# Block-causal attention in front of an MoE and an MLP: from one head in 128-query tiles to two heads in 64-query tiles

## The chip, the cores and the metric

The kernel runs on one core of a Trainium2 chip. The metric is the device time of one launch in microseconds (us). Seven queues of work matter here: PE (TensorE matmuls and transposes) with PEld (its weight loads), DVE (VectorE), ACT (ScalarE), POOL (GpSimd), SP (which only issues DMAs here) and the DMA engines. Each engine executes its own instructions in the order in which the program gives them to it.

## The reference

Attention over 4 batches, 8 heads, 576 positions and 64 columns a head, masked by blocks of 64 positions, then a top-2 MoE over 8 experts, then a gated MLP:

```
B, H, S, D = q.shape                      # 4, 8, 576, 64
scores = 1/sqrt(D) * q @ k^T
mask = (pos[:, None] // 64) >= (pos[None, :] // 64)
scores = where(mask, scores, -1e9);  scores -= max(scores)
attn = exp(scores);  attn /= sum(attn) + 1e-9
x = (attn @ v) -> [B*S, H*D] = [2304, 512]
logits = x @ w_gate + log1p(exp(x @ w_noise)) * noise;  top 2 experts, softmax
out[t] += w * relu(x[t] @ w1[e]) @ w2[e]  # E=8, 512 -> 1024 -> 512
h = x @ w_in;  y = (h * clip(h + 3, 0, 6) / 6) @ w_out    # 512 -> 2048 -> 512
```

## The kernel before

Only the attention stage is changed; it takes about the first 266 us. The MoE and the MLP that follow it are the same text in both kernels.

Values that must be kept close to full fp32 are split in two parts of reduced fp32 (type fp32r), hi = rounded value and lo = value - hi, so that one product is the sum of several fp32r matmuls.

**Unit of work.** Heads come in 16 pairs (two heads of a batch, 128 columns side by side in DRAM), but nearly everything runs head by head. A head's 576 queries are cut in five tiles, `QC`: one of 64 queries and four of 128. A tile sees keys up to its own end: 64, 192, 320, 448, 576.

**q and k.** `hi` and `lo` (L593, L653) split the raw tile of both heads into [hi 64 | lo 64] columns of each head. `prep` (L664 to L671) transposes them on PE, so that hi lies on partitions 0 to 63 and lo on 64 to 127: 20 transposes a pair. `prep_out` (L593, L597) copies PSUM to SBUF (`qk`), on ACT. A swapped copy of q, [lo | hi], called `qw`, is made by two DMAs from POOL's queue (`swap`, L710 and L711); for the first pair PE makes it (`swap_nat`, `swap_prep`).

**Scores** (`scores`, L728). With 128 partitions holding hi and lo, two matmuls (`qk` and `qw` against the same k) give all four products hi*hi, lo*lo, lo*hi, hi*lo. Per head there are 12 matmuls, one or two tiles at a time into the PSUM buffers sb0 and sb1 (units `UN`).

**Mask.** Of a tile of 128 queries, the first 64 must not see the last 64 keys: a DVE memset of -1e30 (L928, four a head) overwrites this corner in PSUM.

**Softmax and P.** `rowmax` (L742, DVE) reduces each tile's scores, `expo` (L749, ACT) writes exp to `P` with the row sums in `rs`. `ptrans` (L767, PE) transposes `P` in 128 x 128 pieces, 15 a head; `pt_hi` (L593, mostly ACT) and `pt_lo` (L786, DVE) split the result into `pth` and `ptl`.

**Output.** `av` (L801, PE) multiplies by v (split by L593 and L653), `av_out` (L593, ACT) copies to `oT`, `fin` (L823, PE) transposes back by a matmul with the identity beside w_gate and w_noise, so that 80 columns come out: 64 of x and 16 of router logits. `x_out` (L831, DVE) divides by the row sum, `lsum` (L842, POOL) adds up the logits over the heads, `store_x` (SP) writes x to DRAM. After the last head of a batch `route` runs some 40 small steps, mostly on DVE.

**The order.** A list scheduler (`Plan`) sets the order in which instructions stand on each engine. `add(engines, fn, deps, prio)` gives a step its possible engines with an assumed cost each, its dependences and a due time; the dictionary `PR` holds the offsets of the due times. Buffers of PSUM (five banks `tb`, sb0, sb1) are handed out by the scheduler. A second plan (`plan2`) follows with the first expert on the first 256 tokens (`s1`, `s2`, L381 to L383), whose x rows were gathered early; it overlaps with the routing of the last batch.

Of the kernel before, what the change touches and what calls it, by code (L numbers as in the profile page):

```python
# [7 lines left out]
F32 = mybir.dt.float32  # L8
# [26 lines left out]
PR = {'split': -19.53, 'prep': -8.13, 'step': 1.69, 'keep': 1, 'S': -0.89, 'max': -12.96, 'exp': 0.81, 'pt': 3.19, 'hi': -5.56, 'lo': -5.14, 'hid': True, 'av': -6.36, 'o': 6.06, 'inv': 0.97, 'fin': 8.98, 'x': -8.39, 'route': 17.77, 'rp': 1, 'route2': 3.35, 'xt': 12, 'eg': 523.9, 'ex': 470.0, 'ew': 2084, 'es': 2041, 'first': 0, 'vpt': (0, 0, 0, 0, 0), 'vhi': (0.8, -0.59, 0.53, -1.31, 2.34), 'vlo': (0.76, -0.19, -0.9, -0.32, -0.13), 'vmax': (0, -1.99, 0, -3.15, 0), 'vexp': (-0.19, 0.18, -0.24, -0.26, -0.46), 'vav': (0.39, 0.71), 'vo': (0.12, -0.03), 'dav': (0.67, 1.02), 'df': 0.98, 'dpt': (0.27, 0.33, 0.44, 0.44, 0.11), 'ds': (0.34, 0.29, 0.4, 0.49), 'sel': 2, 'vh': 0, 'wl': 2, 'wa': 8.24, 'wb': 12.71, 'h': -29.8, 's2': 0.04, 'mask': (1, 2, 3, 4), 'u': (1.2, -1.27, 1.89, -1.62), 'od': True, 'qd': False, 'qa': False}  # L35
# [96 lines left out]
def kernel(  # L132
# [51 lines left out]
    def load(p, nm):  # L184
        src, big, sm, o = {"q": (q, slice(1, NC), 0, BLK), "k": (k_in, slice(0, NC - 1), NC - 1, 0),
                           "v": (v, slice(0, NC - 1), NC - 1, 0)}[nm]
        b, j = pairs[p]
        t = raw[nm, p % 2]
        hs = src[b, 2 * j:2 * j + 2]
        for i in range(2):  # L190
            nc.sync.dma_start(t[:, big, i], hs[i, o:o + S - BLK, :].rearrange("(c p) d -> p c d", p=128))
        r = 0 if o else S - BLK
        nc.sync.dma_start(t[:BLK, sm], hs[:, r:r + BLK, :].rearrange("h p d -> p h d"))

    for nm, pad in (("q", 0), ("k", NC - 1)):
        nc.vector.memset(raw[nm, 0][64:, pad], 0.0)
        load(0, nm)
# [214 lines left out]
    sqk_p = gctx.enter_context(tc.tile_pool(name="sqk", bufs=2, side="right", reuse_waits="tile"))  # L412
# [160 lines left out]
    with actx:  # L573
# [851 lines left out]
```

## Time and profile before

| | us |
|---|---|
| median of 3 runs (1142.65 to 1144.06) | 1144.01 |
| profiled execution | 1144.68 |
| its span, first to last instruction | 1142.9 |
| attention: last `fin` ends | about 266 |

The engines were busy for these shares of the span: PE 98%, DVE 70%, ACT 50%, POOL 25%. Busy time of PE holds the modelled drain of each matmul, so a PE that is 98% busy has hardly a gap, but the duration of one matmul is not what it costs: matmuls overlap. What one costs in a row of matmuls is the distance from its start to the start of the next.

### The profile page before, as it was taken

The numbers are of one execution on the slowest core, as the hardware profiler recorded it, in microseconds if no ns is written. First come the engines' busy times: TensorE is split into PE (matmuls) and PEld (weight loads), VectorE is DVE, ScalarE is ACT, GpSimd is POOL, SyncE is SP. The second block draws the span as 40 slices with busy tenths as digits, with TensorE's granted clock in tenths as the row PEclk, the third lists the DMA queues.
The fourth block names the chain that finished last, engine by engine and source line by source line (L and its number), as shares of the span: only waits on it lengthen the run. The fifth ranks groups of instructions, "written<-read, shape, count | busy, mean of one in ns | idle before, by whom it ended". The sixth has DMA issues, their size and how long they took to land. (4 is left out here: it accounts for less than half of the span.)

```text
span 1142.9 us, 18252 instructions
## 1 busy us (share of the span) xinstructions
PE 1122.8 (98%) x6652; PEld 988.6 (87%) x6652; DVE 803.7 (70%) x1659; ACT 565.9 (50%) x1179; POOL 282.7 (25%) x301
## 2 busy tenths in 40 slices
PE   8999999998999999999999999899999999999998
PEld 6899999997889999999999989788888888888887
DVE  7988999998468788787788775577645554554542
ACT  5888888885442323232323234555444444443442
POOL 5545555435611010101010000275320320200000
PEclk8999999999999999999999999999999999999999
DMA  6865564220697666766655422422101110100000
GB/s 132 199 152 128 130 157 111 64 61 22 223 335 260 246 238 224 250 229 193 205 172 187 172 100 77 155 74 75 46 28 37 29 46 19 38 1 1 38 1 37
DMA packets 134340, 139.71 MB, mean 122 GB/s; under 512 B 67816, under 2 KB 97512, under 8 KB 134248
## 3 DMA queue, kind: packets, MB, share of 16 engines
q1 hardware_dynamic: 118568, 100.30, 28.0%
q0 software_dynamic: 8480, 28.78, 9.2%
q10 hardware_dynamic: 7200, 9.44, 2.3%
q8 instruction: 53, 0.87, 0.3%
q14 instruction: 39, 0.32, 0.1%
HBM read 92.94 MB, written 36.70 MB: 113 GB/s over the span
## 5 line engine op out<-in xcount | busy, mean ns | idle before, releaser
L381 PE MATMUL h<-xh,wah 128*128 128x312 f32 (+5 forms) x832 | 279.9, 336 | 2.9 <-DVE hl L407 2.8
L383 PE MATMUL h<-xh,wal 128*128 128x312 f32 (+5 forms) x832 | 275.1, 331 | 0.0
L382 PE MATMUL h<-xl,wah 128*128 128x312 f32 (+5 forms) x832 | 275.1, 331 | 0.0
L1061 PE MATMUL y<-wbh,hh 128*128 128x512 f32 (+1 forms) x608 | 237.6, 391 | 2.6 <-issue 2.1
L1062 PE MATMUL y<-wbl,hh 128*128 128x512 f32 (+1 forms) x608 | 238.1, 392 | 0.2
L1063 PE MATMUL y<-wbh,hl 128*128 128x512 f32 (+1 forms) x608 | 237.3, 390 | 0.0
L381 PEld LDWEIGHTS h<-xh,wah 128*128 128x128 f32 x832 | 157.5, 189 | 15.2 <-DVE hl L407 3.2
L382 PEld LDWEIGHTS h<-xl,wah 128*128 128x128 f32 x832 | 157.6, 189 | 11.4
L383 PEld LDWEIGHTS h<-xh,wal 128*128 128x128 f32 x832 | 157.5, 189 | 10.3
L1063 PEld LDWEIGHTS y<-wbh,hl 128*128 128x128 f32 (+1 forms) x608 | 113.3, 186 | 25.6 <-DVE hl L1357 0.3
L1061 PEld LDWEIGHTS y<-wbh,hh 128*128 128x128 f32 (+1 forms) x608 | 113.4, 187 | 24.4 <-issue 2.6
L1062 PEld LDWEIGHTS y<-wbl,hh 128*128 128x128 f32 (+1 forms) x608 | 113.3, 186 | 22.3 <-POOL wbl L331 0.8
L404 ACT ACTIVATE hh<-h 128x312 fp32r<-128x312 f32 (+4 forms) x128 | 55.2, 431 | 146.5 <-PE h L383 145.9
L1354 DVE SCALAR_TENSOR_TENSOR r<-r,h 128x512 f32<-128x512 f32 (+1 forms) x80 | 50.5, 632 | 108.6 <-ACT r L1353 108.3
L1353 ACT ACTIVATE r<-h,three 128x512 f32<-128x512 f32 (+1 forms) x80 | 51.6, 644 | 125.8 <-PE h L383 125.8
L1225 POOL DMA_INDIRECT ga<-y_tab,slot x32 | 38.4, 1200 | 294.4 <-PE y L1063 113.7
L1039 POOL DMA_INDIRECT xn<-x_tok,ids x38 | 40.2, 1059 | 268.4 <-PE xps L344 263.9
L331 DVE TENSOR_TENSOR wal<-wa,wah 128x1024 fp32r<-128x1024 f32 x75 | 93.2, 1242 | 16.6 <-ACT wah L327 14.5
L749 ACT ACTIVATE P<-sb,nm 128x320 f32<-128x320 f32 (+4 forms) x160 | 84.8, 531 | 24.4 <-DVE nm L742 20.1
L347 ACT CAST xh<-xps 128x512 fp32r<-128x512 f32 x56 | 32.6, 587 | 127.3 <-PE xps L344 124.7
L331 DVE TENSOR_TENSOR wbl<-wb,wbh 128x1024 fp32r<-128x1024 f32 x71 | 86.5, 1219 | 12.9 <-ACT wbh L327 11.3
L1357 DVE TENSOR_TENSOR hl<-r,hh 128x512 fp32r<-128x512 f32 (+1 forms) x80 | 56.3, 703 | 51.5 <-ACT hh L1356 51.0
(238 smaller groups left out, 1983.1 us busy)
## 6 DMA issues: line engine op xcount, KB each, us to landing
wa<-in_moe_w_dram SPq DMA_DIRECT2D x23, 512.0 KB, 5.4
wb<-in_moe_w_dram SPq DMA_DIRECT2D x23, 512.0 KB, 8.2
qw<-qk POOLq DMA_DIRECT2D x30, 288.0 KB, 4.2
y_tab<-yo SPq DMA_DIRECT2D x32, 256.0 KB, 4.1
w<-in_moe_w_in_dram SPq DMA_DIRECT2D x16, 512.0 KB, 6.7
y_tab<-zero SPq DMA_DIRECT2D x8, 1024.0 KB, 10.9
w<-in_moe_w_out_dram SPq DMA_DIRECT2D x16, 512.0 KB, 5.5
wa<-in_moe_w_dram ACTq DMA_DIRECT2D x9, 512.0 KB, 9.4
```

The lines of the kernel that those rows point to most:

```text
L331: (nc.gpsimd if e == "POOL" else nc.vector).tensor_tensor(lo, raws[PS[u]][which], hi.bitcast(F32), op=OP.subtract)
L381: nc.tensor.matmul(ps, lhsT=wh, rhs=xh, start=first, stop=False)
L382: nc.tensor.matmul(ps, lhsT=wh, rhs=xl, start=False, stop=False)
L383: nc.tensor.matmul(ps, lhsT=wl, rhs=xh, start=False, stop=last)
L404: nc.scalar.activation(h[0][:, c0:c1], ps[:, :c1 - c0], AF.Relu)
L749: nc.scalar.activation(o, views.pop((hd, c)), AF.Exp, bias=nms.pop((hd, c))[:n], scale=1.0, accum_out=rs[hd % 3][:n, c:c + 1])
L1061: nc.tensor.matmul(yps[t][:n], lhsT=hh[:, sl], rhs=wh[:, f % 2], start=first, stop=False)
L1062: nc.tensor.matmul(yps[t][:n], lhsT=hh[:, sl], rhs=wl[:, f % 2], start=False, stop=False)
L1063: nc.tensor.matmul(yps[t][:n], lhsT=hl[:, sl], rhs=wh[:, f % 2], start=False, stop=last)
L1353: nc.scalar.activation(r[:, :n], ps[:, :n], AF.Relu, bias=three, scale=1.0)
L1354: nc.vector.scalar_tensor_tensor(r[:, :n], r[:, :n], 6.0, ps[:, :n], op0=OP.min, op1=OP.mult)
L1357: nc.vector.tensor_tensor(hl[:, :n], r[:, :n], hh[:, :n].bitcast(F32), op=OP.subtract)
```

## The change

The unit becomes a block of 64 queries of both heads of a pair: 128 rows, head 0 in the first 64, head 1 in the last. There are nine blocks a pair, and block i sees 64 (i + 1) keys, so no mask is left.

- q and k: the raw tile of two heads is transposed as it is, unsplit: 10 transposes a pair (4 of q, 4 of k, 2 for the last 64 positions). `prep_out` writes fp32 `qs` and `ks`, on ACT or DVE. Then `q_hi`, `q_lo` split q onto a block diagonal `qd` (head h's 64 partitions, the other head's half of the columns zero; two instructions of 64 partitions each), and `k_hi`, `k_lo` split k. From the second pair on, all four are on POOL alone. The casts of raw q and k on DVE, POOL's subtractions of them and the DMA swap are gone.
- Scores: three matmuls (hi*hi, hi*lo, lo*hi) a block, both heads at once; block 8 in two halves. 30 matmuls a pair.
- P: 25 transposes a pair, nine tiles; `pth` and `ptl` become the tiles `pt`.
- `fin`: 9 matmuls of 96 columns a pair (64 of x, 16 of logits for either head). `lsum` keeps sums of either head's rows in `lgp`, two instructions of 64 partitions a pair; a new `lgm` adds the two halves by three matmuls with a half identity a batch, and `lg_out` copies the result for `route`.
- `store_x` writes 64 partitions by 9 blocks of 64 columns, twice a pair.
- New tiles: `qd`, zeroed by eight memsets on POOL at the start, and `half`. The first expert's weights are split into a pool of their own (`e_p`).
- All due times in `PR` are new.

Its core, with `PR` and the unchanged parts left out:

```diff
+        NB = S // BLK
+        UN = ((0, 1, 3), (2, 4), (5,), (6,), (7,), (8,))
+        PART = ((0, 4), (4, NB))
...
+        qd = [[one.tile([128, NB, 2, BLK], F32R, name=f"qd{i}{w}") for w in "hl"] for i in range(2)]
+        for i in range(2):
+            for t in qd[i]:
+                for h in range(2):
+                    nc.gpsimd.memset(t[64 * h:64 * h + 64, :, 1 - h].bitcast(F32), 0.0)
...
+            if part < 2:
+                for c in range(NC - 1):
+                    nc.tensor.transpose(ps[:, c * 128:(c + 1) * 128], flat("qk"[part], p, c), ident)
+            else:
+                for i, nm in enumerate("qk"):
+                    nc.tensor.transpose(ps[:, i * 128:(i + 1) * 128], flat(nm, p, NC - 1), ident)
...
+        def q_lo(e, p):
+            for h in range(2):
+                r = slice(64 * h, 64 * h + 64)
+                engine(e).tensor_tensor(qd[p % 2][1][r, :, h], qs[p][0][r].rearrange("p (i s) -> p i s", s=BLK),
+                                        qd[p % 2][0][r, :, h].bitcast(F32), op=OP.subtract)
...
-                    for a, kk in enumerate((t, w)):
-                        nc.tensor.matmul(ps[:n, half, o:o + hl], lhsT=kk[:, j, s0:s0 + n],
-                                         rhs=t[:, 2 + j, half * hl:(half + 1) * hl], start=(a == 0), stop=(a == 1))
+                    for a, (w, x) in enumerate(((qh, kh), (qh, kl), (ql, kh))):
+                        nc.tensor.matmul(ps[:, half_, o:o + hl], lhsT=w[:, i], rhs=x[:, ks_], start=(a == 0), stop=(a == 2))
...
+            last = (i1 - 1) // 2
+            for c in range(last + 1):
+                a = max(i0, 2 * c)
+                for w in ((0, 1) if c < last else (1, 0)):
+                    n = 2 * D if w == 0 or (i1 - a) * BLK >= 256 else D
+                    nc.tensor.matmul(o[:n, a - i0:], lhsT=vs[:, c, h, :n], rhs=pt[w][part][:, a - i0:, c, h * BLK:(h + 1) * BLK],
+                                     start=(c == 0 and w == 0), stop=(c == last and w == 0))
...
+            for i in range(i1 - i0):
+                nc.tensor.matmul(f[:, i], lhsT=oT[p, part][:, i].rearrange("p h s -> p (h s)"), rhs=iw[:, p % NP2],
...
+            e1 = {"DVE": 0.7, "ACT": 1.1} if p == 0 else {"POOL": 1.35}
+            e2 = {"DVE": 1.4} if p == 0 else {"POOL": 2.9}
+            f1 = {"ACT": 0.55, "DVE": 0.38} if p == 0 else {"POOL": 0.68}
+            f2 = {"POOL": 1.45, "DVE": 0.68} if p == 0 else {"POOL": 1.45}
...
+            k["qh", p] = add(e1, lambda e, p=p: q_hi(e, p), [outs[0], outs[2]] + sold, tp)
+            k["ql", p] = add(e2, lambda e, p=p: q_lo(e, p), [k["qh", p]], tp)
+            k["kh", p] = add(f1, lambda e, p=p: k_hi(e, p), [outs[1], outs[3]] + sold, tp)
+            k["kl", p] = add(f2, lambda e, p=p: k_lo(e, p), [k["kh", p]], tp)
```

`sold` holds the six score units of the pair two before, since `qd` has two buffers.

What stands on POOL for one pair in the middle of the stage, before (`sp_q`, `sp_k`, `sp_v` are the split tiles, L710 and L711 the swap's DMAs, L842 the logit sum):

```order
L593 CAST sp_v<-raw_v_76 128x10x64
L653 TENSOR_TENSOR sp_v<-raw_v_76,sp_v 128x10x64
L653 TENSOR_TENSOR sp_q<-raw_q_73,sp_q 128x10x64
L653 TENSOR_TENSOR sp_k<-raw_k_75,sp_k 128x10x64
L842 TENSOR_TENSOR lg_158<-lg_158,x 128x80
L710 DMA qw<-qk 64x1152
L711 DMA qw<-qk 64x1152
L842 TENSOR_TENSOR lg_158<-lg_158,x 128x80
```

And after the change, again on POOL for one pair (`qd0h`, `qd0l`, `kh`, `kl` are the split q and k after the transposes):

```order
L580 CAST sp_v<-raw_v_76 128x10x64
L580 CAST qd0h<-qs 64x9x64 x2
L808 TENSOR_TENSOR lgp_219<-lgp_219,x 64x144 x2
L684 TENSOR_TENSOR qd0l<-qs,qd0h 64x9x64 x2
L580 CAST kh<-ks 128x576
L648 TENSOR_TENSOR sp_v<-raw_v_76,sp_v 128x10x64
L692 TENSOR_TENSOR kl<-ks,kh 128x576
```

The split of q and k has moved behind the transposes, and its casts have moved from DVE to POOL.

At the start of the program POOL has this before (`pth`, `ptl` take memsets; `sp_v` of the first pair is the first subtraction):

```order
L621 MEMSET P_195 128x64
L625 MEMSET rs_197 64x1
L625 MEMSET rs_199 64x1
L625 MEMSET rs_201 64x1
L629 MEMSET pth 64x128
L629 MEMSET ptl 64x128
L653 TENSOR_TENSOR sp_v<-raw_v_76,sp_v 128x10x64
L653 TENSOR_TENSOR sp_q<-raw_q_73,sp_q 128x10x64
```

and after, in the same place on POOL (`kl` in the third row from the end belongs to the first pair):

```order
L612 MEMSET qd1l 64x9x64 x2
L617 MEMSET P_194 128x64
L617 MEMSET P_197 128x64
L617 MEMSET P_200 128x64
L617 MEMSET P_203 128x64
L617 MEMSET P_206 128x64
L622 MEMSET half 128x192
L624 COPY half<-ident 64x64 x2
L648 TENSOR_TENSOR sp_v<-raw_v_76,sp_v 128x10x64
L692 TENSOR_TENSOR kl<-ks,kh 128x576
L580 CAST qd1h<-qs 64x9x64 x2
L580 CAST kh<-ks 128x576
```

The first pair's `kl`, which all its scores need, now stands on POOL behind the memsets and behind `sp_v`; before, nothing that the first scores need was on POOL.

At the end of the stage PE has this before (`raw_k_74` holds early gathered token rows, `h` is the first expert's product):

```order
L344 MATMUL tb_178<-ident,raw_k_74 128x128 x4
L801 MATMUL tb_179<-pth,sp_v 128x256
L801 MATMUL tb_179<-ptl,sp_v 128x256
...
L823 MATMUL tb_180<-iw,oT_4128 64x80
L823 MATMUL tb_180<-iw,oT_4128 128x80 x2
L823 MATMUL tb_180<-iw,oT_4157 128x80 x2
L381 MATMUL h<-xh,wah 128x256
```

and this after:

```order
L790 MATMUL tb_174<-iw,oT_3572 128x96 x4
L790 MATMUL tb_172<-iw,oT_3566 128x96 x5
L337 MATMUL tb_175<-ident,raw_q_72 128x128 x4
L337 MATMUL tb_171<-ident,raw_k_74 128x128 x4
L813 MATMUL tb_173<-lgp_220,half 128x16
L814 MATMUL tb_173<-lgp_220,half 128x64
L815 MATMUL tb_173<-lgp_220,half 128x64
L366 MATMUL h<-xh,wah 128x256
```

The transposes of the early token rows have moved behind the last `fin`, directly ahead of the expert that needs them, and the three matmuls of `lgm` stand between.

## Rows read from the trace of the kernel before

**Rows 1.** Windows: us, busy us (instructions) of each engine, clock, DMA share, GB/s.
```profile
10.00:20.00 10.00, 8.17 (x50) 7.01 (x50) 9.64 (x25) 6.50 (x20) 7.46 (x6) 0.83 0.62 137
20.00:30.00 10.00, 8.34 (x58) 7.68 (x56) 7.51 (x19) 6.53 (x20) 4.38 (x5) 0.83 0.66 133
40.00:256.00 216.00, 214.01 (x1797) 200.79 (x1795) 196.20 (x642) 182.41 (x561) 109.25 (x148) 1.00 0.52 124
```
**Rows 2.** Groups by form, DVE in 40 to 256 us: count | busy, mean ns | idle.
```profile
L742 DVE TENSOR_REDUCE nm<-sb 128x1 f32<-128x576 f32 x28 | 21.0, 748 | 0.3
L928 DVE MEMSET sb<- 64x64 f32 x113 | 12.7, 112 | 11.7 <-PE sb L728 9.5 <-ACT oT L593 1.0
```
**Rows 3.** Timeline of PE, two heads: start us, us to the end, what.
```profile
152.69 0.28 PE L801 MATMUL tb<-pth,sp_v 128*128 128x256 f32 x1
152.81 0.28 PE L801 MATMUL tb<-ptl,sp_v 128*128 128x256 f32 x1
...
153.29 0.34 PE L801 MATMUL tb<-ptl,sp_v 128*128 128x256 f32 x2
153.47 0.27 PE L801 MATMUL tb<-pth,sp_v 128*128 128x128 f32 x1
153.57 0.20 PE L728 MATMUL sb<-qk 128*64 128x64 f32 x1
...
153.95 0.33 PE L801 MATMUL tb<-pth,sp_v 128*128 128x320 f32 x1
154.12 0.31 PE L801 MATMUL tb<-ptl,sp_v 128*128 128x320 f32 x1
154.27 0.27 PE L801 MATMUL tb<-pth,sp_v 128*128 128x256 f32 x1
...
154.98 0.29 PE L728 MATMUL sb<-qk 128*128 128x288 f32 x1
155.11 0.29 PE L728 MATMUL sb<-qk,qw 128*128 128x288 f32 x1
...
155.35 0.60 PE L664 MATMUL tb<-ident,sp_q 128*128 128x128 f32 x4
155.79 0.49 PE L767 MATMUL tb<-ident,P 128*128 128x128 f32 x3
...
156.32 0.36 PE L728 MATMUL sb<-qk,qw 128*128 128x448 f32 x1
156.52 0.60 PE L767 MATMUL tb<-ident,P 128*128 128x128 f32 x4
...
157.44 1.40 PE L823 MATMUL tb<-iw,oT 128*64 128x80 f32 x10
158.63 0.39 PE L728 MATMUL sb<-qk 128*128 128x320 f32 x1
```
**Rows 4.** Groups by form, POOL in 40 to 256 us.
```profile
L653 POOL TENSOR_TENSOR sp_v<-raw_v,sp_v 128x640 fp32r<-128x640 f32 x13 | 20.5, 1578 | 0.6
L842 POOL TENSOR_TENSOR lg<-lg,x 128x80 f32<-128x80 f32 x25 | 9.0, 359 | 13.8 <-DVE x L831 9.8 <-DVE sb L928 2.2 <-DMA raw_v<-in_v_dram 0.9
L593 POOL CAST sp_v<-raw_v 128x640 fp32r<-128x640 f32 x12 | 8.7, 722 | 11.9 <-PE tb L801 11.8
L520 POOL TENSOR_TENSOR rid<-ohs,bw 128x400 bf16<-128x400 f32 x6 | 5.1, 861 | 0.0
```
**Rows 5.** Timeline of the start, POOL and PE.
```profile
4.08 0.20 POOL L629 MEMSET pth<- 64x128 f32 x1
...
9.10 1.55 POOL L653 TENSOR_TENSOR sp_v<-raw_v,sp_v 128x640 fp32r<-128x640 f32 x1 [4.68 <-ACT sp_v L593]
9.75 0.42 PE L728 MATMUL sb<-qk 128*128 128x320 f32 x1
```
**Rows 6.** Timeline of the end of the attention stage: POOL, DVE, PE.
```profile
264.24 0.69 DVE L352 TENSOR_TENSOR xl<-tb,xh 128x512 fp32r<-128x512 f32 x1 [0.48 <-ACT xh L347]
...
266.14 2.42 POOL L331 TENSOR_TENSOR wal<-wa,wah 128x1024 fp32r<-128x1024 f32 x1 [1.88 <-ACT wah L327]
266.63 2.03 DVE L842 TENSOR_TENSOR lg<-lg,x 128x80 f32<-128x80 f32 x1
271.75 0.39 PE L381 MATMUL h<-xh,wah 128*128 128x256 f32 x1 [2.81 <-DVE hl L407]
```

More of the change, by code (lines that the diff above doesn't have):

```diff
@@ L724, in scores @@
                 nh = 1 if L <= 512 else 2
                 hl = L // nh
-                for half in range(nh):
-                    for a, kk in enumerate((t, w)):
-                        nc.tensor.matmul(ps[:n, half, o:o + hl], lhsT=kk[:, j, s0:s0 + n],
-                                         rhs=t[:, 2 + j, half * hl:(half + 1) * hl], start=(a == 0), stop=(a == 1))
-                        if a == 0 and c and c not in PR["mask"] and half == nh - 1:
-                            nc.tensor.matmul(ps[:n, half, o + hl - BLK:o + hl], lhsT=mneg, rhs=ones[0:1, 0:BLK],
-                                             start=False, stop=False)
@@ new lines, in x_out, with lsum @@
+        def x_out(g, p, part, cols=slice(0, FW)):
+            if p not in xt:
+                xt[p] = sm_p.tile([128, NB, FW], F32, tag="x", name="x", bufs=3)
+            i0, i1 = PART[part]
+            nc.vector.tensor_tensor(xt[p][:, i0:i1, cols], fview(g, part)[:, :, cols],
+                                    ri[p][:, i0:i1, None].to_broadcast([128, i1 - i0, cols.stop - cols.start]), op=OP.mult)
+        def lsum(e, p):
+            b, j = pairs[p]
+            for h in range(2):
+                r = slice(64 * h, 64 * h + 64)
+                t = xt[p][r, :, D + h * 2 * E:D + (h + 1) * 2 * E]
+                if j == 0:
+                    engine(e).tensor_copy(lgp[b % 2][r], t)
+                else:
+                    engine(e).tensor_tensor(lgp[b % 2][r], lgp[b % 2][r], t, op=OP.add)
@@ L850, in load_noise, with store_x @@
+        def store_x(p):
+            b, j = pairs[p]
+            for h in range(2):
+                d = (2 * j + h) * D
+                nc.sync.dma_start(x_tok[b * S:(b + 1) * S, d:d + D].rearrange("(i r) d -> r i d", r=BLK),
+                                  xt[p][64 * h:64 * h + 64, :, 0:D])
         def load_noise(b):
@@ L871 @@
                 add({"SP": 1.1}, lambda e, p=p: load_raw(RAWP.index(p) + 1), [k["L", "v", p]], u0 + 4)
[L872 to L883 removed]
+            vu = u0 + PR["v"]
@@ L957 @@
                 g = Bank("t", 1)
-                k["F", hd] = add({"PE": PR["df"]}, lambda e, g=g, hd=hd: fin(g, hd), [k["O", hd, 0], k["O", hd, 1]],
-                                 U + PR["fin"], take=g)
-                old = [k.get(("X", b - 2, r)) for r in range(NP2)] + [k.get(("ls", 8 * (b - 1) - 1))] if h == 0 else []
-                cut = D if last else 0
+                k["F", p, part] = add({"PE": 0.222 * n}, lambda e, g=g, p=p, part=part: fin(g, p, part),
+                                      [k["O", p, h, part] for h in range(2)], U + PR["fin"] + PR["vf"][part], take=g)
```

517 lines of the change are left out of this document (206 added, 311 removed).

## The prediction

> **What bounds the kernel now.** First the busy time of each engine by stretches [rows 1]. From 40 to 256 us, where the pairs follow one another without start or tail, PE is busy for 214 of 216 us at full clock, DVE for 196, ACT for 182, POOL for 109. Next, groups by form: a group that runs once a head has a count of 28 there (`rowmax` of the full 576 keys [rows 2]). So a head takes 216 / 28 = 7.71 us and a pair 15.43. Last, the timeline of PE [rows 3]: its rows overlap (a matmul that starts at 152.69 and lasts 0.28 is followed by one at 152.81), so what a matmul costs is the distance to the next start. The stage is bound by the number and width of PE's matmuls. DVE at 91% is the second, and POOL has 49% to spare. The stages behind the attention run the same text and are taken as unchanged.
>
> **The change part by part: PE in a pair.** Costs by distance of starts, from [rows 3]:
>
> - A transpose of 128 columns: 155.35 to 155.79 for four, 0.11 each. Of 64 columns: 0.06, the value that the low half of 128 leaves in 153.29 to 153.47 (0.18, less 0.12 for the 256 columns before it).
> - AV: 256 columns 0.12, 320 columns 0.17 and 0.15, 128 columns 0.10 and 0.06.
> - Scores: the tiles of 64 and 192 keys take 153.57 to 153.95 for four matmuls, 0.38; 288 keys 0.13; 448 keys 0.20; 320 keys 0.15.
> - `fin` is full fp32, and each of its five matmuls a head stands twice in the trace: ten take 157.44 to 158.63, 1.19.
>
> Before, per pair: preparation 16 x 0.11 + 4 x 0.06 = 2.0. Scores of a head 0.38 + 0.30 + 4 x 0.13 + 2 x 0.20 = 1.60, so 3.2. P 30 x 0.11 = 3.3. AV of a head 10 x 0.12 + 0.32 (two of 320) + 4 x 0.08 = 1.84, so 3.7. `fin` 2.4. Together 14.6; the 0.8 that is left of 15.43 is route, switches and small gaps, and I keep it.
>
> After: preparation 10 x 0.11 = 1.1. P 25 x 0.11 = 2.75. `fin` 9 matmuls, 18 rows of 0.119 = 2.14. Scores, three matmuls a block: 0.11 for 64, 128 and 192 keys, 0.12 for 256, 0.15 for 320, 0.175 for 384 (between its neighbours), 0.20 for 448, 0.23 for 512 (carried on), 0.26 for 576; sum 1.465, times three 4.40. AV of a head by the order: two of 256 columns, six of 320, two each of 192, 128 and 64, so 0.24 + 0.90 + 0.20 + 0.16 + 0.16 = 1.66, a pair 3.3. Together 13.7. The scores grow by 1.2; preparation, P, AV and `fin` shrink by 0.9, 0.55, 0.35 and 0.25. Net -0.85 a pair.
>
> Unknown is the 64-key score matmul with 128-wide weights and a start of its own: at 0.06 (the narrow one above) it saves 3 x 2 x 0.05 = 0.3 a pair more, at 0.13 it costs 0.2 more. I take 0.11, the transposes' value, since these too have 128-wide weights. `lgm` is three full fp32 matmuls a batch, so six rows, at 0.11 to 0.119 (the widths lie beside `fin`'s): 4 x 6 x 0.11 = 2.6 us. Sixteen pairs: -13.6 + 2.6 = -11, with -5 to -16 from the 64-key bounds and a tenth of the 0.8 a pair either way. I take -12.5, since fewer and larger steps (nine score blocks for ten tiles, no mask between scores and `rowmax`) leave fewer switches.
>
> The Trainium skill, "TensorE: Matmul & The Clock Gate", section "Back-to-back issue gap", gives 81 ns a matmul for 128 columns and 131 for 512 in a sustained stream. By it (linear between, an estimate) a pair would go from 11.1 to 10.0 and the stage would gain 15 us in place of 11. The rows show 110 ns for 128 columns and 200 for 448, and 15.4 a pair; the measurement decides, and the sum above uses it.
>
> **The other engines in a pair.** DVE loses eight masks a pair (four a head, 113 in 28 heads [rows 2]) of 0.112 = 0.9 us, two casts, one `rowmax`; its 14.0 a pair (196.2 / 14) falls to about 12.5, and ACT loses copies. That takes nothing off the end: it loosens the cover. POOL gains [rows 4]: v cast 0.72 and subtraction 1.58 stay; new are q's casts 2 x 0.65 and k's 0.65 (0.72 x 576 / 640), q's subtractions 2 x 1.42 and k's 1.42 (1.578 x 576 / 640), logit sums about 1.0 for two of 144 columns (0.359 for 80), and route's steps such as 0.861. Sum 9.5 + 1.2 = 10.7 a pair, against PE's 14.6. No trace shows an operation on 64 partitions of POOL with a block stride. Bounds: half of the full-width row, when partitions count (half of the 4.1 of q goes: 8.6 a pair), and 1.5 times it, for the stride (the blocks written are not contiguous), which gives 10.7 + 0.5 x 6.2 = 13.8 or, if all of POOL stretches likewise, 16.05. I take the row itself, since a cost per column is what the 640 and 80 columns on 128 partitions show. Then a pair's split takes 6.2 us in a row, of two pairs' 14.6 that it may be early (two buffers of `qd`): hidden. If that cover is gone, each pair costs what POOL exceeds PE by.
>
> **The start.** Before, the first score matmul comes at 9.75, beside POOL's first subtraction (9.10, 1.55 [rows 5]). After, all first-pair scores need `kl`, which stands on POOL behind that subtraction: 9.10 + 1.55 + 1.42 + 0.15 = 12.2, +2.5. Ahead of it stand the eight `qd` memsets of 64 x 576 (four rows of x2); a 64 x 128 one took 0.20 [rows 5], so they cost between 8 x 0.2 = 1.6 and, by columns, 8 x 0.9 = 7.2. POOL idled for 4.68 ahead of 9.10; I take 8 x 0.55 = 4.4, hidden; by columns first scores come at 13.6, +3.8. Against that: between 10 and 30 us PE started 50 + 58 = 108 matmuls at clock 0.83 [rows 1], where 10 us of the steady stretch hold 1797 / 21.6 = 83, so 58 fewer; at 0.12 each that is 7 us of fill. The change brings a longer run of scores a pair and no split ahead of the transposes; I give back 3 of these 7 (0 to 7). Start: +2.5 - 3 = -0.5, from +3.8 to -4.5.
>
> **The tail.** Eight token transposes (0.88), their copies on ACT and the 0.69 of `xl` on DVE [rows 6] move behind the last `fin`, with `lgm` and its copy ahead of route. Before, the expert's matmul at 271.75 followed 2.81 of idle time [rows 6], so part is hidden. Between -1 (all in that gap, the last pair shorter) and +5 (0.88 + 0.69 + copies + 0.66 of `lgm` + a wait for POOL of 2.42); I take +2. What waits there is DVE, in order: its logit sum took 2.03 us from 266.63 and ended at 268.66, with POOL's `wal` (266.14 + 2.42 = 268.56 [rows 6]), while the same operation took 0.359 on POOL [rows 4]. The Trainium skill, "SBUF — State Buffer", section "Who interferes with whom", calls the port pair that DVE and GpSimd share "an exclusive lock". The trace agrees with it there, and it speaks against more work on POOL: the waits that it would bring are part of the third case below.
>
> Sum: -12.5 - 0.5 + 2 = -11, so the profiled 1144.68 would become 1133.7; the profiled run lies 0.67 above the median, and against the median's 1144.01 it is 1133. I forecast **1133 us**.
>
> **The rivals.** *The bound stays on PE and shrinks* (the forecast): 1124 to 1139, from the bounds above without the far ends of POOL. For it speaks a PE that is 99% busy; against it, that DVE is at 91%, so more than 1.4 us a pair could not be taken off by PE alone.
>
> *POOL becomes the bound.* The q and k split of the next pair gates its scores, and PE waits at the first block of each pair. It reaches PE's 14.6 at 14.6 / 10.7 = 1.36 times my rows, and the old 15.43 at 1.44 times. At 1.5 times it is 16.05 a pair, (16.05 - 15.43) x 16 = +10, and the start's `kl` comes later too (nothing gained there): about 1154. For it: strided writes on half the partitions, and the six operations in a row. Against: the rows are for the same types, and POOL is idle for half the time now.
>
> *PE's gain turns into waits of its own.* Fewer score buffers' worth of steps in flight, and DVE in order: a `rowmax` behind an operation that is held by POOL keeps a score buffer 1.4 us (one subtraction) longer. Half of that once a pair, 0.7 x 16 = 11, eats the gain on PE: 1143, between 1138 and 1148. For it: POOL's share of time rises from 51% to 10.7 / 14.6 = 73%. Against: PE has other work (P, AV) to put there.
>
> *More is gained.* The 64-key matmuls go at 0.06 (-5), the fill is recovered whole (-4), and the tail costs nothing (-2), with half of the switches gone (-4): 1118, from 1110 to 1124. For it: 58 matmuls short in the fill. Against: each of these is the favourable end.
>
> **How the numbers follow.** Chances: forecast 0.54, POOL 0.18, waits 0.15, more 0.13. Within 0.2% (2.3 us, what a measurement of this kernel can tell from no change) lie 1141.7 to 1146.3. The forecast and the last case lie wholly on the faster side (0.67), the POOL case on the slower side (0.18); the waits split in 0.06 faster, 0.06 same and 0.03 slower. So faster 0.73, same 0.06, slower 0.21. The range 1117 to 1151 leaves out about a third of the last case and the larger half of POOL's; the likeliest case's own is 1124 to 1139.
>
> **What would show it.** Right: a pair in 14.3 to 14.9 us between 40 and 250 us, PE still over 97% busy there, POOL near 10.7 a pair with subtractions of 64 x 9 x 64 near 1.42, `kl` of the first pair ending near 12, first scores behind it, and the first expert matmul at 259 to 263. Wrong: those subtractions above 2.0 with PE idle ahead of the first score of a pair, released by POOL (the second case); PE idle in pieces under 1 us, released by DVE or by score buffers (the third); 64-key score matmuls at 0.06 (the fourth). A first score later than 14 us, or an expert matmul that comes over 9 us after the last `fin`, would put the error in the start or the tail.

## The result and the profile after

| | before | after |
|---|---|---|
| median of 4 runs, same chip | 1143.33 us (1141.16 to 1144.06) | 1131.46 us (1129.82 to 1132.65) |
| ratio | | 0.9898 (0.9877 to 0.9920) |
| profiled execution | 1144.68 us | 1132.54 us |
| last `fin` ends | 266.04 us | 251.06 us |
| first product of the expert's second weight, `y` | 276.21 us | 265.22 us |

The change takes 1.0% off: 11.9 us by the medians and 12.1 by the profiled executions, where 11 was forecast. The attention ends 15.0 us earlier, the stretch from there to the first `y` product is 4.0 us longer (14.2 for 10.2), and what follows is 1.1 shorter. The profiled execution is one of the slower two of the four runs (1132.5 and 1132.7 us at a mean granted clock of 0.987; the other two took 1129.8 and 1130.4 at 0.993).

The first `y` is not the same point in both orders: after the change the route's matmuls `rps` stand ahead of it, before they stood behind six `y` products. At the next point that both kernels reach with the same work done, the matmul `cps` of the MoE (336.03 us before, 325.55 after), PE is 10.5 us ahead, so that 4.5 of the 15.0 are lost by then. From `cps` to the end the same text took 803.0 to 806.9 us in the fourteen profiled executions of this document, 1.6 less after than before, which lies within that spread.

The stretches of [rows 1], now in the kernel after (us, then busy us and instructions of PE, PEld, DVE, ACT, POOL, then clock, DMA share, GB/s):

```profile
10.00:20.00 10.00, 8.35 (x33) 6.97 (x34) 8.27 (x14) 3.58 (x14) 9.45 (x9) 0.50 0.71 161
20.00:30.00 10.00, 10.00 (x70) 9.61 (x70) 6.72 (x14) 8.07 (x24) 4.88 (x6) 0.85 0.43 78
40.00:256.00 216.00, 209.67 (x1688) 201.84 (x1687) 174.85 (x467) 153.17 (x480) 140.52 (x175) 0.99 0.38 88
```

DVE and ACT are looser, POOL fuller, and PE has a few us of gaps that it did not have before. Where they lie is seen from the times at which the widest `rowmax`, once a pair now, starts on DVE (start us, us, what; the first line belongs to the third pair, the last to the last):

```profile
46.64 0.76 DVE L716 TENSOR_REDUCE nm<-sb 128x1 f32<-128x576 f32 x1 [1.03 <-PE sb L708]
...
115.11 0.76 DVE L716 TENSOR_REDUCE nm<-sb 128x1 f32<-128x576 f32 x1
...
128.79 0.76 DVE L716 TENSOR_REDUCE nm<-sb 128x1 f32<-128x576 f32 x1
...
145.22 0.74 DVE L716 TENSOR_REDUCE nm<-sb 128x1 f32<-128x576 f32 x1
...
237.12 0.75 DVE L716 TENSOR_REDUCE nm<-sb 128x1 f32<-128x576 f32 x1
```

And before, for the second head of the third pair and of the last:

```profile
56.85 0.74 DVE L742 TENSOR_REDUCE nm<-sb 128x1 f32<-128x576 f32 x1
...
256.12 0.76 DVE L742 TENSOR_REDUCE nm<-sb 128x1 f32<-128x576 f32 x1
```

After the change one pair takes 13.7 us, the next one 16.4. So it goes on: from 60 to 129 us a pair takes 13.7 to 13.9 (one 14.1), with PE busy all the time; the seven pairs from 128.8 to 237.1, in which the routes of batches 1 and 2 fall, take 15.5 on the mean. Over the 13 pairs from the third to the last that is 14.65 a pair; before it was 15.33.

PE at two score blocks in one of the short pairs (512 keys, then 64):

```profile
102.85 0.45 PE L708 MATMUL sb<-kh,qd0h 128*128 128x512 f32 x1
103.13 0.39 PE L708 MATMUL sb<-kl,qd0h 128*128 128x512 f32 x1
103.36 0.40 PE L708 MATMUL sb<-kh,qd0l 128*128 128x512 f32 x1
...
108.78 0.28 PE L708 MATMUL sb<-kh,qd1h 128*128 128x64 f32 x1
108.89 0.28 PE L708 MATMUL sb<-kl,qd1h 128*128 128x64 f32 x1
```

The 64-key matmul costs 0.11, the value taken. The first wide matmul of a group costs more than the next (0.28 against 0.23), which the forecast had left in its rest of 0.8. And POOL, by form, 40 to 240 us:

```profile
L684 POOL TENSOR_TENSOR qd1l<-qs,qd1h 64x576 fp32r<-64x576 f32 x14 | 20.0, 1428 | 0.9
L692 POOL TENSOR_TENSOR kl<-ks,kh 128x576 fp32r<-128x576 f32 x13 | 18.6, 1429 | 0.7
...
L580 POOL CAST kh<-ks 128x576 fp32r<-128x576 f32 x13 | 8.6, 664 | 0.8
```

On 64 partitions a subtraction takes 1.43 us, on 128 the same: POOL's price goes by the columns, as [rows 4] had suggested.

**The start.** The kernel after, first 17 us, engines together:

```profile
2.94 1.19 POOL L612 MEMSET qd0h<- 64x576 f32 x2
...
9.19 1.54 POOL L648 TENSOR_TENSOR sp_v<-raw_v,sp_v 128x640 fp32r<-128x640 f32 x1
9.31 3.91 DVE L684 TENSOR_TENSOR qd0l<-qs,qd0h 64x576 fp32r<-64x576 f32 x2
9.90 1.09 PE L658 MATMUL tb<-ident,raw_q 128*128 128x128 f32 x4 [2.82 <-DMA raw_q<-in_q_dram]
10.69 1.91 POOL L692 TENSOR_TENSOR kl<-ks,kh 128x576 fp32r<-128x576 f32 x1
...
12.09 0.45 PE L661 MATMUL tb<-ident,raw_k 128*128 128x128 f32 x1 [0.89 <-DMA raw_k<-in_k_dram]
12.33 1.06 PE L658 MATMUL tb<-ident,raw_k 128*128 128x128 f32 x4
13.05 0.40 PE L708 MATMUL sb<-kh,qd0h 128*128 128x64 f32 x1
13.26 0.40 PE L708 MATMUL sb<-kl,qd0h 128*128 128x64 f32 x1
...
15.33 1.29 DVE L256 CAST tab<-tidi 128x20 bf16<-128x20 int32 x1
16.93 0.41 DVE L716 TENSOR_REDUCE nm<-sb 128x1 f32<-128x64 f32 x2
```

`kl` ends at 12.60 and the first scores come at 13.05, 3.3 later than before [rows 5]; the memsets cost 0.6 each. But `kl` was not the last thing that these scores stood behind. In PE's order the second pair's transposes come first, and for their k PE waited until 12.09 on a load; and DVE's `qd0l`, which the third product needs, took 3.91 us beside POOL's two subtractions and ended at 13.22. Two more things were not foreseen: the first `rowmax` waits until 16.93, behind six steps that build constants for the route, and PE, which stood idle for 2.82 us up to 9.90, runs at a granted clock of 0.50 from 10 to 20 us, that is at 1.2 GHz, where a 64-key matmul takes 0.21.

**The tail.** The same kernel behind the last `fin`:

```profile
253.75 2.39 POOL L324 TENSOR_TENSOR wal<-wa,wah 128x1024 fp32r<-128x1024 f32 x1 [3.17 <-ACT wah L320]
253.96 0.39 PE L366 MATMUL h<-xh,wah 128*128 128x256 f32 x1 [0.44 <-DVE xl L345]
254.42 1.78 DVE L427 TENSOR_TENSOR zx<-zx,noise 128x40 f32<-128x40 f32 x1
256.08 2.40 POOL L324 TENSOR_TENSOR wbl<-wb,wbh 128x1024 fp32r<-128x1024 f32 x1
256.23 2.31 DVE L427 TENSOR_TENSOR zx<-zx,lg 128x40 f32<-128x40 f32 x1
...
262.54 2.43 POOL L324 TENSOR_TENSOR wbl<-wb,wbh 128x1024 fp32r<-128x1024 f32 x1
262.79 2.23 DVE L427 TENSOR_TENSOR ohb<-ohs 128x40 bf16<-128x40 f32 x1
265.07 0.18 PE L471 MATMUL rps<-ohb,before 128*128 128x40 bf16 x1 [2.73 <-DVE ohb L427]
```

Three DVE steps on 40 columns, which take 0.2 elsewhere, end each with a subtraction of POOL, as the logit sum did in [rows 6]. Such waits are not new, though. The kernel before, in the same part:

```profile
265.83 0.36 PE L381 MATMUL h<-xh,wah 128*128 128x256 f32 x1
...
272.93 2.31 DVE L442 TENSOR_TENSOR nl<-nl,zx 128x40 f32<-128x40 f32 x1
...
278.34 0.18 PE L486 MATMUL rps<-ohb,before 128*128 128x40 bf16 x1 [0.57 <-DVE ohb L442]
```

There the logit sum (2.03), `zx` (1.90), `nl` (2.31) and `dl` (1.25) took 7.5 us together; after the change `zx` twice, `dl` (1.06) and `ohb` take 7.4. What is new is PE's order. The expert's first product came at 265.83 before, 0.2 ahead of the end of the last `fin`, and comes 2.9 behind it now (253.96); and `rps`, which needs `ohb`, stands ahead of the first `y`, so that PE waits 2.73 for it in place of 0.57.

### The profile page after: what moved, and what is told of

Its sections match the earlier page's. It is cut to its first block, busy times and chain, and to the rows that moved or that the text cites. A ratio compares the mean times of both kernels' runs of the same rounds, so it can differ in the third digit from the quotient of the medians.

```text
span 1130.8 us, 17329 instructions
## 1 busy us (share of the span) xinstructions
PE 1106.3 (98%) x6426; PEld 981.4 (87%) x6426; DVE 767.4 (68%) x1432; ACT 525.9 (47%) x1074; POOL 315.0 (28%) x333
## 5 line engine op out<-in xcount | busy, mean ns | idle before, releaser
L366 PEld LDWEIGHTS h<-xh,wah 128*128 128x128 f32 x832 | 157.9, 190 | 14.4 <-DVE hl L392 0.9
L1007 PEld LDWEIGHTS y<-wbh,hh 128*128 128x128 f32 (+1 forms) x608 | 113.9, 187 | 24.1 <-issue 2.6
L1008 PEld LDWEIGHTS y<-wbl,hh 128*128 128x128 f32 (+1 forms) x608 | 113.9, 187 | 21.6
L324 DVE TENSOR_TENSOR wbl<-wb,wbh 128x1024 fp32r<-128x1024 f32 x71 | 86.6, 1220 | 13.4 <-ACT wbh L320 10.7
L722 ACT ACTIVATE P<-sb,nm 128x576 f32<-128x576 f32 (+4 forms) x144 | 75.4, 530 | 39.7 <-DVE nm L716 37.0
L320 ACT CAST wbh<-wb 128x1024 fp32r<-128x1024 f32 x80 | 84.0, 1050 | 17.7 <-PE y L1009 16.3
```

The lines of the kernel that those rows point to most:

```text
L320: nc.scalar.copy(w_s[which, u][0], raws[PS[u]][which])
L324: (nc.gpsimd if e == "POOL" else nc.vector).tensor_tensor(lo, raws[PS[u]][which], hi.bitcast(F32), op=OP.subtract)
L366: nc.tensor.matmul(ps, lhsT=wh, rhs=xh, start=first, stop=False)
L722: nc.scalar.activation(o, views.pop((p, i)), AF.Exp, bias=nms.pop((p, i)), scale=1.0, accum_out=rs[p % 3][:, i:i + 1])
L1007: nc.tensor.matmul(yps[t][:n], lhsT=hh[:, sl], rhs=wh[:, f % 2], start=first, stop=False)
L1008: nc.tensor.matmul(yps[t][:n], lhsT=hh[:, sl], rhs=wl[:, f % 2], start=False, stop=False)
```

## The experiments

Theory: in most pairs PE's matmuls set the time; in the pairs with a route on DVE (batches 1 and 2) it is DVE, and much of what it lacks there is time in which POOL's split holds it. Rivals: POOL's split itself gates the scores; the route's own work, POOL or not; and for start and tail, that other waits take the place of those named. One rival has no run: all due times in `PR` are new, and no run gives the kernel before a new set of its own. What a schedule tuned again would have given it stays open; a later due time for one step (e4) and two other offsets (e7) moved the kernel after by -2.6 and +6.1 us here.

Medians against runs of the kernel before on the same chip; "to after" is the difference of the ratio from 0.9898, in us of 1143.3. The interval of the ratio after (0.0021 either way) goes into it, so that it is known to about 3 us.

| run | median us | ratio (95%) | to after, us |
|---|---|---|---|
| e1 no low q | 1125.63 | 0.9844 (0.9831 to 0.9857) | -6.2 |
| e2 low q twice | 1150.17 | 1.0058 (1.0043 to 1.0073) | +18.3 |
| e3 route on POOL | 1127.53 | 0.9868 (0.9854 to 0.9882) | -3.4 |
| e4 constants later | 1129.06 | 0.9875 (0.9859 to 0.9891) | -2.6 |
| e5 fourth pass | 1144.98 | 1.0024 (1.0015 to 1.0033) | +14.4 |
| e6 before, no masks | 1141.18 | 0.9990 (0.9980 to 1.0000) | |
| e7 token transposes first | 1137.80 | 0.9951 (0.9938 to 0.9964) | +6.1 |
| e8 three together | 1123.99 | 0.9832 (0.9819 to 0.9845) | -7.5 |
| e9 casts on ACT | 1141.11 | 0.9992 (0.9983 to 1.0001) | +10.7 |
| e10 weights on DVE | 1128.62 | 0.9885 (0.9870 to 0.9899) | -1.5 |
| e11 route, constants, casts | 1131.31 | 0.9899 (0.9885 to 0.9914) | 0 |
| e12 four together | 1125.83 | 0.9848 (0.9831 to 0.9866) | -5.7 |

### POOL's share: e1, e2

```diff
 def q_lo(e, p):
-    for h in range(2):
+    for h in range(2 if p < 2 else 0):                    # e1
+    for h in (0, 1) if p == 0 else (0, 1, 0, 1):          # e2
```

> From the third pair on the low part of q is not computed any more (the two buffers keep what the first two pairs wrote), so the output's low bits are wrong; PE, DVE, ACT and all orders stay. POOL loses two subtractions of 64 x 576 a pair, 2 x 1.43 = 2.9 us. Theory (around the route steps, pairs 8 to 11 and 12 to 15, DVE's instructions are held by POOL's subtractions, and P's low part comes late to PE): the pairs between 128 and 237 us come down from 15.5 on the mean towards 14.5, 3 to 7 us less in all; the undisturbed pairs stay at 13.7. Rival 1 (the route's own work on DVE takes the time, whoever runs on POOL): within 1 us of the changed kernel. Rival 2 (POOL's split gates the scores everywhere): the undisturbed pairs fall below 13.7 too, over 8 us less.

> From the second pair on POOL computes the low part of q twice (same values): 2.9 us more a pair, 10.7 to 13.6, just under PE's 13.7. Theory (POOL harms by holding DVE, and most where DVE has no time to spare): undisturbed pairs stay at 13.7 to 14.0, pairs around the route lose 1 to 2 us each, 6 to 14 us more in all. Rival 1 (POOL touches nothing until it is full): 0 to 2 us more. Rival 2 (POOL is already the gate): 2.9 x 15 = 43 us more.

A view of the route in the kernel after, DVE, POOL and PE around 143 us:

```profile
142.51 2.46 DVE L509 TENSOR_SCALAR sel<-laneb,pmf 128x128 bf16<-128x128 bf16 x2
143.35 1.57 POOL L648 TENSOR_TENSOR sp_v<-raw_v,sp_v 128x640 fp32r<-128x640 f32 x1
144.89 0.41 DVE L755 TENSOR_TENSOR ptl<-tb,pth 128x256 fp32r<-128x256 f32 x1
145.36 0.39 PE L766 MATMUL tb<-pth,sp_v 128*128 128x256 f32 x1 [0.69 <-DVE ptl L755]
145.89 1.38 DVE L509 TENSOR_SCALAR sel<-laneb,pmf 128x128 bf16<-128x128 bf16 x8
```

Eight `sel` steps take 1.38 where nothing is on POOL, and two take 2.46 beside `rid` and `sp_v`, ending with `sp_v` at 144.9; `ptl` stands behind them, and PE waits 0.69 for it. The Trainium skill, "SBUF — State Buffer", section "Who interferes with whom", says that casts and `tensor_scalar` steps can use the port pair shared with GpSimd, and `tensor_reduce` on this chip never does. The trace agrees: the `rowmax` at 145.22 took 0.74 like all others, though POOL's second `rid` ran beside it until 145.74.

A wait that e1 takes away, first in the kernel after, then in e1, where POOL is done with `kl` at 139.3:

```profile
140.52 1.43 POOL L692 TENSOR_TENSOR kl<-ks,kh 128x576 fp32r<-128x576 f32 x1
140.59 1.54 DVE L427 TENSOR_TENSOR bt<-pt,eio 128x25 f32<-128x25 int32 x2
```

```profile
140.86 0.28 DVE L427 TENSOR_TENSOR bt<-pt,eio 128x25 f32<-128x25 int32 x2
```

The stretch from 128 to 237 us in the kernel after, then in e1, then in e2:

```profile
128.00:237.00 109.00, 104.01 (x830) 98.86 (x828) 94.61 (x271) 74.21 (x236) 69.97 (x91) 0.98 0.28 63
```

```profile
128.00:237.00 109.00, 106.39 (x876) 102.13 (x875) 94.20 (x283) 78.30 (x247) 50.73 (x75) 1.00 0.28 63
```

```profile
128.00:237.00 109.00, 95.36 (x738) 92.13 (x737) 89.66 (x212) 66.33 (x210) 84.33 (x93) 0.94 0.29 65
```

In e1 the undisturbed pairs stay at 13.7 and the seven later pairs take 103.2 us in place of 108.3: 5.1 of the 6.2 come from there, as the theory has it. The `sel` steps above wait as before (2.43), since `sp_v` stays. Part of the 5.1 is PE's clock. In the kernel after PE waits 0.41 and then 1.11 us (for `P` and `ptl`) up to 206.55, and then the granted clock stands at 0.50 for a while:

```profile
206.00:212.00 6.00, 5.45 (x27) 4.51 (x28) 4.44 (x12) 4.17 (x11) 2.15 (x4) 0.72 0.00 0
```

In e1 it is 1.00 in the whole stretch. Six us at 0.72 are 1.7 us of PE's work less (an estimate from this row); so some 3.4 of the 5.1 are left for the waits themselves. In e2 pairs stay at 13.7 until 101 us, then most take 16 to 20. POOL had 10.0 us in a short pair after the change (64.2 of 88 us from 40 to 128); with 2.9 more and the route's steps the split falls behind for good. That is worse than the theory's 6 to 14 and far from the 43 of a POOL that gates already. PE's clock (0.94 in the stretch shown) has a part in it as well. How much of it is DVE held and how much late scores isn't settled; PE's waits there are for P (ACT) and `ptl` (DVE).

### The route's small steps: e3

```diff
-PR = {... 'rp': 1, ...}
+PR = {... 'rp': 3, ...}
```

`rp` is the number of batches whose small route steps may stand on POOL.

> The small elementwise steps of the routes of batches 1 and 2 go to POOL, where those of batch 0 already are; the planner then shifts some neighbours. The route of batch 0 falls in pairs that take 13.7 us, those of batches 1 and 2 in pairs of 15.5. Theory (DVE instructions with two SBUF inputs wait for POOL, so that moving a dozen of them a batch to POOL takes these waits off DVE): the pairs from 128 to 237 us come down by 3 to 8 us in all. Rival (what costs there are the sel and reduce steps, which stay on DVE, or the batch's number alone): within 1.5 us.

The seven pairs took 101.4 us (108.3 after), so 6.9 are won there, the clock's 1.7 among them (it is 1.00 from 206 to 212 us in e3); by the first `y` product (261.6 for 265.2) about half of it is left, the rest went in the last pair and the tail. The theory's size is right in the trace; the time alone (3.4, known to 3) would not have shown it. With the steps their waits leave DVE too, so e3 does not tell the steps' own time from the waits.

### The start: e4

```diff
-        k["tab"] = add({"DVE": 0.9}, lambda e: tables(), [], 3, after=12.0)
+        k["tab"] = add({"DVE": 0.9}, lambda e: tables(), [], 3, after=40.0)
```

> Six small steps that build constants for the route stand on DVE between the first q split and the first rowmax (13.25 to 16.5 us); here they are due later, PE's order is unchanged. Theory (at the start the first rowmax waits for DVE, which those steps hold): first rowmax at 13.3 to 14 in place of 16.93, 2 to 3.5 us less in all. Rival (PE's clock of 0.5 and the loads of the second pair decide the fill): first rowmax earlier, but the end moves by under 1 us.

The first `rowmax` in e4:

```profile
15.31 0.42 DVE L716 TENSOR_REDUCE nm<-sb 128x1 f32<-128x64 f32 x2 [0.48 <-PE sb L708]
```

The first `rowmax` comes 1.6 us earlier, less than expected, since it now waits for PE's scores, whose last product in that unit starts at 14.86 (14.90 in the kernel after): 1.6 was all that the six steps held. The first pair's widest `rowmax` comes at 21.6 (24.1 after), and the end moves by about as much. The start varies between executions, though: with the six steps in their old place (after, e1, e2, e3, e7, e10) that `rowmax` comes at 22.6 to 24.3 us, with the steps later (e4, e8, e12) at 21.2 to 21.6. So the gain there is 1.0 to 3.1.

### PE as the bound: e5, and the masks of before: e6

```diff
-for a, (w, x) in enumerate(((qh, kh), (qh, kl), (ql, kh))):
+for a, (w, x) in enumerate(((qh, kh), (qh, kl), (ql, kh), (ql, kl))):   # e5, with stop=(a == 3)
```

```diff
-ms = add({"DVE": 0.075}, lambda e, hd=hd, c=c: nc.vector.memset(tails.pop((hd, c)), NEG), [ms], ...
+ms = add({"DVE": 0.075}, lambda e, hd=hd, c=c: tails.pop((hd, c)) and None, [ms], ...     # e6, on the kernel before
```

> Every score block of the changed kernel gets a fourth matmul (lo*lo, which the three passes leave out); all other engines keep their orders. By the distances of the kl matmuls in the trace (0.111 for 64 keys to 0.234 for 512, 0.264 for 576; sum 1.48 a pair) it is 1.48 x 16 = 23.7 us of PE. Theory (PE sets the end, and only some of the waits around the routes can hide it): 18 to 24 us more, the undisturbed pair at 15.2 in place of 13.7. Rival (the second half is set by DVE, so that PE's work is free there): 8 to 13 us more, the pairs from 128 to 237 us as long as without it.

> The kernel before, without its 128 memsets that mask the corners (scores of masked keys stay in, so the output is another); PE's order is unchanged. Theory (the masks were hidden behind PE, as costed at nothing on the path): within 2 us of the kernel before. Rival (the memset between scores and rowmax held a score buffer, and that is where the 0.8 us a pair went that the sum of the matmuls left): 6 to 13 us less than before.

Two widest `rowmax` steps of e5:

```profile
108.22 0.76 DVE L716 TENSOR_REDUCE nm<-sb 128x1 f32<-128x576 f32 x1 [0.42 <-PE sb L708]
...
123.37 0.76 DVE L716 TENSOR_REDUCE nm<-sb 128x1 f32<-128x576 f32 x1 [0.43 <-PE sb L708]
```

A short pair goes from 13.7 to 15.2, by the full 1.48 of the added matmuls; a pair in the route's stretch from 15.5 to 15.9 only, since PE has gaps there. So neither expectation was right for the whole (14.4 between 13 and 18): PE sets the short pairs. In the route's stretch of the kernel after it waits 4.7 us in all, 2.8 of them for DVE and the rest for ACT. e6 lies 1.1 us below the kernel before: the masks were hidden, as the forecast had costed them.

### The tail: e7, e10

```diff
-PR = {... 'eg': 537.67, 'ex': 466.81, ... 'wl': 2, ...}
+PR = {... 'eg': 95.0, 'ex': 106.0, ... }      # e7
+PR = {... 'wl': 0, ...}                       # e10
```

> The eight transposes of the early token rows go back ahead of the last fin, and the two xl steps of DVE ahead of the last x_out. Theory (0.87 of PE work goes into the gap ahead of the last fin and 1.29 of DVE off the chain from the last fin to the expert): first expert matmul at about 252 in place of 253.96, 1.5 to 3 us less in all. Rival (the next stop is the route, whose DVE steps wait for POOL's wal and wbl): the expert starts earlier and waits longer, under 0.8 us less.

DVE, POOL and PE of e7 behind the last `fin`:

```profile
252.87 2.35 POOL L324 TENSOR_TENSOR wal<-wa,wah 128x1024 fp32r<-128x1024 f32 x1 [1.95 <-ACT wah L320]
253.72 4.03 DVE L808 TENSOR_TENSOR lgp<-lgp,x 64x144 f32<-64x144 f32 x2
255.17 4.79 POOL L324 TENSOR_TENSOR wbl<-wb,wbh 128x1024 fp32r<-128x1024 f32 x2
257.80 0.61 PE L813 MATMUL tb<-lgp,half 128*128 128x16 f32 x2 [4.76 <-DVE lgp L808]
```

Both expectations failed: it is 6.1 us slower. The edit let ACT and POOL start on the weights 0.9 us earlier, before DVE's two `lgp` steps; each then waited for a POOL subtraction, and `lgm`, which stands ahead of the expert on PE, waited for them: first expert matmul at 259.10 in place of 253.96. In the kernel after, the same two steps took 0.63, just ahead of POOL. Not all of the loss lies there: from the last `fin` to `cps` e7 takes 78.8 us, 4.3 more than the kernel after, and the last `fin` itself ends 2.0 later (253.04). One pair (204.8 to 222.1 us) took 17.3 for 15.5, with a granted clock of 0.57 from 206 to 214 us (0.79 after); that the edit caused this is not shown.

> The first expert's weights are split on DVE (about 1.2 us each) where the planner has POOL do it (2.4 each) beside the last route; attention stays. In the changed kernel the route's steps zx, zx, dl and ohb took 1.78, 2.31, 1.06 and 2.23 there, where they take about 0.2 alone: 6.6 us of waiting, and PE waited 2.73 for ohb. Theory (these waits set the stretch from the last fin to the first y product): first y product at 10 to 12.5 us after the last fin in place of 14.2, 1.5 to 4 us less in all. Rival (DVE is the bound there whoever splits, since it takes on 4 to 5 splits of 1.2): within 1 us, or slower.

From the logits to the positions the long waits are gone but one (`u`, 2.26 us), and DVE has the splits of 1.2 us in their place. 1.5 us less, within the uncertainty: the theory is not shown by the time. The first `y` came 5.9 us after the last `fin`, earlier than the 10 to 12.5 expected, since PE now has it ahead of `rps`. From the last `fin` to `cps` e10 took 71.6 us in place of 74.5; but e12, with the same edit, took 74.3 where e8 took 71.8. So what the splits on DVE give depends on the order around them.

### Together, and where it fails: e8, e9, e11, e12

e8 is e3, e4 and e7 in one; e12 adds e10. e9 moves the casts, e11 is e3, e4 and e9:

```diff
-e1 = {"DVE": 0.7, "ACT": 1.1} if p == 0 else {"POOL": 1.35}
-f1 = {"ACT": 0.55, "DVE": 0.38} if p == 0 else {"POOL": 0.68}
+e1 = {"DVE": 0.7, "ACT": 1.1} if p == 0 else {"ACT": 1.1}
+f1 = {"ACT": 0.55, "DVE": 0.38} if p == 0 else {"ACT": 0.55}
```

> The full computation with three edits together: the route's small steps of batches 1 and 2 on POOL, the constants' steps later, the token transposes ahead of the last fin. Theory (three separate places, so the gains add up): 3.9 + 2.4 + 1.5 to 3 = 8 to 9 us less than the changed kernel, about 1123. Rival (an earlier start meets the same waits later): 4 to 6 us less.

> The full computation; from the second pair on the casts of q and k (qh, kh) are on ACT in place of POOL: POOL loses 3 x 0.66 = 2.0 us a pair, ACT gains about 1.65 (it is busy 11 of 13.7 now near the front, 9.7 on the mean), and the planner moves some PSUM copies from ACT to DVE. Theory (time goes where POOL holds DVE in the route's pairs, and the undisturbed pair is PE's): undisturbed pairs stay at 13.7 to 13.9, the pairs from 128 to 237 us lose 2 to 4 us in all, 1127 to 1129.5. Rival (with ACT's and DVE's copies later, P comes late to PE in every pair): 14.2 or more in the undisturbed pairs, 3 to 8 us slower than the changed kernel.

> The full computation with the route's small steps of batches 1 and 2 on POOL, the constants' steps later and the q and k casts on ACT. Theory (the first two edits added up before; the third takes POOL's load away where the route's steps have added to it): 1131.4 - 3.9 - 2.4 - 2 = about 1123, between 1121 and 1125. Rival (casts on ACT shift the bound of the undisturbed pair): 1127 or more.

> The full computation: the route's small steps of batches 1 and 2 on POOL, the constants' steps later, the token transposes ahead of the last fin, and the first expert's weights split on DVE beside the last route, so that POOL holds no DVE step there. Theory (in the run of the first three PE still waited 3.3 us for the expert's low part on DVE, behind route steps held by POOL): 1.5 to 3 us less than those three, 1121 to 1122.5. Rival (DVE is full there either way): 1123.5 or more.

e8 is the fastest full computation here: 0.9832 of the kernel before, 7.5 us below the change alone, between the sum and its rival. Its parts are not those of the sum: e7's edit, which costs 6.1 by itself, does not cost there (PE waited 1.0 us for `lgp`, and 3.3 later for the expert's low part): from the last `fin` to `cps` e8 takes 71.8 us, 2.7 less than the kernel after. e12 gains nothing more, as its rival said; the rival's reason, that DVE is full at that place, was not tested by itself. e9 fell to its rival, and beyond its 3 to 8 us. So did e11: the route's steps and the constants gain 6.0 by their own runs, and with the casts on ACT nothing of it is left (1131.3). The largest group of PE's waits in e9, 20 to 280 us (total, times, longest):

```profile
PE tb L658 <- DVE ptl L755: 2.8, 7, 0.6
```

The planner, with ACT fuller, gave DVE more copies, and the four pairs from 48.0 to 109.0 us took 15.3 each, where no pair but those of the route had been slow. The waits do not explain that: in these 61 us PE waits 1.0 for `ptl` and idles for 1.3 in all, of some 6 that the four pairs lose. The order of PE moved as well in e9, so its 10.7 us are not the casts' alone, and their cause stays open.

## Why the prediction was right, and which terms were off

- **PE in a pair** (-12.5 taken, -11 by the sum): the mean of the 13 pairs fell by 0.68, and the sixteen, nine short ones and seven with a route, take 9 x 13.7 + 108.3 = 231.6 us where 16 x 15.33 = 245.3 stood before: -13.7. The sum came near that for a reason that it did not contain. It gave 13.7 of matmuls and kept 0.8 of "route, switches and gaps" in every pair. The short pairs have 13.7 and no rest; that the matmuls alone come to 13.7 is two errors that cancel, since wide groups cost more at their first matmul (the scores of a pair took 4.9 us, not 4.4) and transposes less (25 of P took 2.43, not 2.75, by the distances of starts summed from 101.4 to 115.1). The pairs with a route have a rest of 1.8, and nearly half the gain that sixteen short pairs would have given is lost there. The rival "PE's gain turns into waits" named a mechanism for this (DVE held by POOL) and spread it over all pairs; e1 shows it in the seven, for some 3.4 us of the 12.4 that they take above 7 x 13.7, and the clock, which fell there in the kernel after and not in e1, for 1.7 more. Where the other 7 come from is not shown.
- **The other engines**: masks hidden (e6), POOL at its rows' price, 10.0 us a short pair for 10.7. "POOL becomes the bound" did not occur, but e2 shows it lies less than 2.9 us a pair away.
- **The start** (-0.5, from +3.8 to -4.5): up to the last `fin` 15.0 us were won; less the pairs' 13.7, start and last pair together gave 1.3, and the two were not measured apart. `kl` came as forecast (12.60 for 12.2), but it was one of three steps that ended late, with the load of the second pair's k and `qd0l`. The 3 us of fill that the sum gave back are not seen: by the sum's own count PE started 33 + 70 = 103 matmuls from 10 to 30 us, where 20 us of its steady stretch hold 2 x 1688 / 21.6 = 156, so 53 are missing (58 before).
- **The tail** (+2, from -1 to +5): +4.0 to the first `y`, +4.5 to `cps`. The list of steps was right, but the expert's product at 271.75, from which the gap of 2.81 was read, is its 25th; the first stood at 265.83, with no gap to hide in. The 25th came at 259.24, within the 259 to 263 that the forecast gave for "the first". The waits of DVE for POOL, which the far end of the range counted as new (2.42), were there before to the same amount; the wait for `ohb` ahead of the first `y` was not in the sum.
- Everything behind the first `y` product had been taken as unchanged and is 1.1 us shorter; from `cps` on the difference lies within what the same text varies by.

So the errors are -1.2 in the pairs, -0.8 in start and last pair, +2.0 in the tail and -1.1 behind. They nearly cancel, and that the total came within about 1 us is luck in part: the sum gave every pair 14.6, and what ran is nine of 13.7 and seven of 15.5.

## What to carry to other kernels

A stretch that one engine bounds has a period; look at it pair by pair, not by its mean, since a mean of 14.65 was made of 13.7 and 15.5: a fourth score pass lengthened the short pairs by its full time and the others by 0.4 (e5). When work moves to GpSimd, its own spare time is not the whole price: each of its subtractions can hold a short VectorE step for nearly its full length (`zx` 2.31 us beside `wbl`, 0.2 elsewhere), and the price is paid where VectorE has no slack. And a step taken off a chain's end may start its neighbour earlier, which then stands in the way (e7).

## What the runs showed of the hardware

- GpSimd on 64 partitions is as slow as on 128: 1428 ns and 1429 ns for 576 columns, casts 663 and 664.
- A score matmul of 64 columns with 128-wide weights takes 0.11 us of PE at full clock, as one of 128 does behind the first of its block; at a granted clock of 0.50 it is 0.21 (13.05 to 13.26).
- DVE's `lgp` step on 64 x 144 took about 2 us beside two GpSimd subtractions and 0.3 just ahead of them (4.03 and 0.63 for two).
- Behind a stop of 2.82 us of PE the granted clock was 0.50 from 10 to 20 us. Behind two waits of 0.41 and 1.11 us close together (up to 206.55) it was 0.50 again, from 208 to 210 us, and a score matmul of 512 columns took 0.42 us (207.40 to 207.82) in place of 0.23. In e1 PE idled for 0.55 of the 6 us from 204.6 to 210.6, and the clock stayed at 1.00.
